# Emptying a group's accumulators before the next group's gate sums, and a new order of the last products

## The chip, the cores and the metric

The kernel runs on one core of a Trainium2 chip. The metric is device time in microseconds (us) from start to end of one execution. Of before, three runs are shown: median 794.53 us, from 793.96 to 796.04. Beside them stands one execution taken by the hardware profiler, which lasted 793.31 us; its trace spans 791.2 us from the first to the last instruction, and 2.1 us lie around it.

## What is computed

The reference runs three stages over 3072 tokens of 384 numbers: a recurrent attention, a mixture of eight experts with a skip score, and a dense feed-forward layer with a gate. Only the last is touched by the change:

```python
def _moe2_ref(x, w_in, w_out):          # x 3072x384, w_in 384x2048, w_out 2048x384
    h = x @ w_in
    g = h * (1.0 / (1.0 + np.exp(-h)))
    return (g @ w_out).astype(np.float32)
```

Sums are kept near float32 accuracy: each factor is split in a high and a low part (names ending in h and l), and a product is three matmuls, high by high, low by high and high by low (`product`, all at L934).

## The kernel before

The dense layer takes the tokens in six groups of 512. The 2048 inner columns are 16 blocks of 128. For each block f, `up` makes the sums of the gate (9 matmuls of 512 columns into a bank `ph`, two of which rotate), and `silu` makes the gate value g on ScalarE (L1201), its high part gh on ScalarE (L1202) and its low part gl on VectorE (L1203). I call that last step the gate subtraction.

Groups 0 and 1 then multiply plainly (`down`), into four banks y0 to y3, which `store` copies out at the end (L1371, two copies on VectorE and two on ScalarE), for an indirect store from GpSimd. These four banks are the ones that the next group needs.

Groups 2 to 5 (`seven`) save matmuls: blocks f = p and f = p + 8 form a pair, and of the product of a 2 by 2 arrangement (two blocks of the inner dimension, two halves of 256 tokens, two d tiles of the output) seven products are made in place of eight. For each pair, `pair` and `pair_split` make differences of gates and split them (VectorE L1215, L1224, L1226, ScalarE L1223; tiles tz and twd). TensorE then runs:

- `plain`: two products into the halves of bank y0 (3 matmuls of 256 columns each), `third` (the output's third d tile, which is multiplied plainly: 6 matmuls of 512 columns into bank `pd`) and a product of the gate's second half into y2[:, 1], with weights `sw`;
- `mixed`: four products, 12 matmuls of 256 columns, into both halves of y1, into y2[:, 0] and into y3[:, 0].

All eight pairs accumulate in the same banks. When the last pair is through, `out_plain` (ScalarE copy L1271, VectorE L1272), `out_third` (ScalarE L1276) and `out_mixed` (six VectorE additions, L1283 to L1288) combine the banks into the tile o, and `store` sends it off. Each pool tag y0 to y3 has one buffer, so the next group can't open a bank before the last reader of the same bank is through.

The order is written by times: `at(time, fn, ...)` puts a step in a list that is sorted by time, and each engine executes its own instructions in that order. Q is a group's start in these units, a pair takes PE_P = 7.44, and `lag` = Q + 8 PE_P is the start of the next group. The next group's block 0 is at `lag`, its block 8 at lag + PE_P/2 with its `silu` 2 later, `pair` at lag + PE_P/2 + 2.6 and `pair_split` at 3.2. In between stand the last pair's `plain` (lag + 1.9) and `mixed` (lag + PE_P/2 + 1.9), and `out_mixed` at lag + PE_P/2 + 3.3, that is, behind `pair_split` of the next group. In the last group (`end`), `third` of pairs 6 and 7 is taken out of `plain` and put behind the last `mixed`; its bank is copied out in two halves (L1278 on ScalarE, L1279 on VectorE), and two stores follow, both from SyncE's queue.

Of the kernel before, what the change touches and what calls it, by code (L numbers as in the profile page):

```python
# [949 lines left out]
def dense(tc, k, outer):  # L950
# [240 lines left out]
    def seven(g, Q, u, up):  # L1191
# [40 lines left out]
        def add(out, w, x, p, start, stop):  # L1232
            (wh, wl), (xh, xl) = w, x
            product(nc, out, [(wh, xh), (wl, xh), (wh, xl)], p == 0 and start, p == 7 and stop)
# [8 lines left out]
            u.y = [ps.tile([128, 2, 256], F32, name="py", tag="y%d" % n) for n in range(4)]  # L1243
            u.d = ps.tile([128, 512], F32, name="pd", tag="t", bufs=2)

        def plain(p):
            if p == 0:
                open_banks()
            add(u.y[0][:, 0], weights(p, 0), gate(p, 0), p, True, False)
            add(u.y[0][:, 1], weights(p + 8, 0), gate(p + 8, 0), p, False, True)  # L1250
            if not (end and p > 5):
                third(p)
            add(u.y[2][:, 1], sums(p, 3), gate(p + 8, 1), p, True, False)

        def third(p):
            for f in (p, p + 8):
                (wh, wl), xh, xl = weights(f, 2), u.gh[f], u.gl[f]
                product(nc, u.d, [(wh, xh), (wl, xh), (wh, xl)], f == 0, f == 15)

        def mixed(p):  # L1260
            add(u.y[1][:, 0], sums(p, 1), u.t[1], p, True, False)
            add(u.y[1][:, 1], sums(p, 2), u.t[2], p, False, True)
            add(u.y[2][:, 0], sums(p, 0), u.t[0], p, False, True)
            add(u.y[3][:, 0], weights(p + 8, 1), u.t[3], p, True, True)

        def half(j, n):
            return u.o[:, j, 256 * n:256 * n + 256]
# [4 lines left out]
            tt(half(0, 0), u.y[0][:, 1], half(1, 1), ALU.add)  # L1272

        def out_third():
            if not end:
                nc.scalar.copy(u.o[:, 2], u.d)  # L1276
                return
            nc.scalar.copy(half(2, 0), u.d[:, 0:256])  # L1278
            nc.vector.tensor_copy(half(2, 1), u.d[:, 256:512])  # L1279

        def out_mixed():
            p1 = half(1, 1)
            tt(half(0, 1), u.y[1][:, 0], p1, ALU.add)  # L1283
            tt(half(1, 0), u.y[1][:, 1], half(0, 1), ALU.add)
            tt(half(0, 1), u.y[2][:, 0], half(0, 1), ALU.add)
            tt(half(1, 1), u.y[2][:, 0], half(1, 0), ALU.add)
            tt(half(0, 1), u.y[2][:, 1], half(0, 1), ALU.add)
            tt(half(1, 0), half(1, 0), u.y[3][:, 0], ALU.subtract)  # L1288

        def store(a, b):  # L1290
            o = k.out[g * 512:g * 512 + 512, :].rearrange("n d -> (n d)").rearrange("(j p t) -> p j t", j=3, p=128)
            nc.sync.dma_start(o[:, a:b], u.o[:, a:b])

        u.g = [None, None]
        for p in range(8):
            t = Q + PE_P * p
            for i in range(2):
                at(t + PE_P * i / 2, up, p + 8 * i)
                at(t + PE_P * i / 2 + 2, silu, p + 8 * i)
            at(t + PE_P / 2 + 2.6, pair, p)  # L1300
            at(t + PE_P / 2 + 3.2, pair_split, p)
            at(t + PE_P + 1.9, plain, p)
            at(t + PE_P * 1.5 + 1.9, mixed, p)
        at(lag + 1.95, out_plain)
        at(lag + PE_P / 2 + 3.3, out_mixed)
        if not end:
            at(lag + 1.96, out_third)
            at(lag + PE_P, store, 0, 3)
            return
        at(lag + PE_P / 2 + 1.91, third, 6)  # L1310
        at(lag + PE_P / 2 + 1.92, third, 7)
        at(lag + PE_P, store, 0, 2)
        at(lag + PE_P + 0.1, out_third)
        at(lag + PE_P + 0.2, store, 2, 3)

    def group(g, Q):
        u = Ctx()
# [69 lines left out]
        for f in range(16):  # L1387
# [1 line left out]
            at(t, up, f)  # L1389
            at(t + 2, silu, f)  # L1390
            at(t + 2 * PE_F + 2, down, f)
        at(Q + 18 * PE_F, store)
    sw = {}
    order = k.const.tile([128, 8], U32, name="order")

# [364 lines left out]
```

## Time and profile before

| what | of before |
|---|---|
| median of three runs | 794.53 us (793.96 to 796.04) |
| profiled execution | 793.31 us, span of its trace 791.2 us |
| TensorE busy | 750.2 us, 95% of the span |
| VectorE, ScalarE, GpSimd busy | 536.6, 437.9 and 230.1 us |
| mean granted TensorE clock | 0.982 |
| the chain of work that ended last | TensorE 75%, VectorE 12%, DMA 6%, ScalarE 3% |

The busy time of TensorE counts matmuls from start to modelled end, and consecutive ones overlap; what to look for is where a stretch has idle time, and at which clock the matmuls behind it run. In the timeline rows below, the text in brackets gives how long the engine had been idle ahead of an instruction and whom it waited for. L numbers are lines of the kernel.

### The profile page before, as it was taken

The numbers are of one execution on the slowest core, as the hardware profiler recorded it, in microseconds if no ns is written. First come the engines' busy times: TensorE is split into PE (matmuls) and PEld (weight loads), VectorE is DVE, ScalarE is ACT, GpSimd is POOL, SyncE is SP. The second block draws the span as 40 slices with busy tenths as digits, with TensorE's granted clock in tenths as the row PEclk, the third lists the DMA queues.
The fourth block names the chain that finished last, engine by engine and source line by source line (L and its number), as shares of the span: only waits on it lengthen the run. The fifth ranks groups of instructions, "written<-read, shape, count | busy, mean of one in ns | idle before, by whom it ended". The sixth has DMA issues, their size and how long they took to land.

```text
span 791.2 us, 13883 instructions
## 1 busy us (share of the span) xinstructions
PE 750.2 (95%) x5471; PEld 686.1 (87%) x5471; DVE 536.6 (68%) x952; ACT 437.9 (55%) x718; POOL 230.1 (29%) x199
## 2 busy tenths in 40 slices
PE   2899999999989999999999999999999999999996
PEld 2799999998879999998899999978878887887884
DVE  7898899999556668679996345555555566465544
ACT  8899889954334554445774212345544454454543
POOL 5577657132536334452300148420000000000000
PEclk8699999999999999999999999999999999999998
DMA  8668685597659755566750010011010101101001
GB/s 341 182 184 272 223 294 177 176 255 219 210 186 327 274 192 180 199 235 205 239 161 1 20 61 1 1 41 41 1 41 1 41 1 40 41 1 41 1 1 44
DMA packets 31372, 101.88 MB, mean 129 GB/s; under 512 B 4929, under 2 KB 13249, under 8 KB 31297
## 3 DMA queue, kind: packets, MB, share of 16 engines
q1 hardware_dynamic: 26112, 88.31, 34.0%
q0 software_dynamic: 3072, 9.44, 3.3%
q10 hardware_dynamic: 2112, 3.15, 1.3%
q8 instruction: 45, 0.74, 0.4%
q14 instruction: 31, 0.25, 0.1%
HBM read 69.27 MB, written 12.58 MB: 103 GB/s over the span
## 4 chain that ended last, share of the span: by engine, by line
PE 75%; DVE 12%; DMA 6%; ACT 3%; issue 2%; SPq 2%; DVEq 0%; ACTq 0%
PE ph L934 29%; PE py L934 23%; PE pd L934 5%; PE sc L481 4%; DMA KQ<-o 4%; PE run L308 2%; PE pu L514 2%; PE py L499 2%; PE py L503 2%; SPq L445 1%; DMA raw<-in_w_dram 1%; PE tp L471 1%; PE ph L924 1%; DVE wl L1011 1%; DVE o L242 1%
## 5 line engine op out<-in xcount | busy, mean ns | idle before, releaser
L934 PE MATMUL ph<-cxh,wh 128*128 128x512 f32 x288 | 116.1, 403 | 0.0
L1203 DVE TENSOR_TENSOR gl<-g,gh 128x512 fp32r<-128x512 f32 x64 | 44.3, 692 | 103.4 <-ACT gh L1202 103.4
L934 PE MATMUL ph<-cxl,wh 128*128 128x512 f32 x288 | 114.3, 397 | 0.1
L934 PE MATMUL ph<-cxh,wl 128*128 128x512 f32 x288 | 114.2, 396 | 0.0
L1201 ACT ACTIVATE g<-ph 128x512 f32<-128x512 f32 x64 | 38.2, 597 | 68.8 <-PE ph L934 68.6
L934 PEld LDWEIGHTS ph<-cxl,wh 128*128 128x128 f32 x288 | 54.9, 191 | 13.2 <-DVE cxl L1344 0.5
L934 PEld LDWEIGHTS ph<-cxh,wl 128*128 128x128 f32 x288 | 55.2, 192 | 8.7
L934 PEld LDWEIGHTS ph<-cxh,wh 128*128 128x128 f32 x288 | 55.0, 191 | 8.4
L1223 ACT CAST tz<-twd 128x256 fp32r<-128x256 f32 x96 | 36.7, 407 | 36.8 <-DVE twd L1215 36.7
L481 PE MATMUL sc<-KQ 96*128 96x128 f32 x384 | 53.0, 286 | 1.0 <-DMA KQ<-o 0.8
L481 PEld LDWEIGHTS sc<-KQ 96*128 96x128 f32 x384 | 47.8, 198 | 3.3 <-issue 1.4
L1011 DVE TENSOR_TENSOR wl<-raw,wh 128x1536 fp32r<-128x1536 f32 x22 | 43.2, 1973 | 10.5 <-ACT wh L915 10.5
L915 ACT CAST wh<-raw 128x1536 fp32r<-128x1536 f32 x28 | 40.8, 1480 | 15.2 <-DMA raw<-in_w_dram 15.2
L934 PE MATMUL ph<-xh,wh 128*128 128x256 f32 x168 | 47.9, 285 | 0.0
L934 PE MATMUL ph<-xl,wh 128*128 128x256 f32 x168 | 47.6, 283 | 0.0
L934 PE MATMUL ph<-xh,wl 128*128 128x256 f32 x168 | 47.6, 283 | 0.0
L934 PE MATMUL py<-wh,gl 128*128 128x384 f32 x128 | 43.3, 338 | 0.0
L934 PE MATMUL py<-wh,gh 128*128 128x384 f32 x128 | 43.2, 338 | 0.0
L934 PE MATMUL py<-wl,gh 128*128 128x384 f32 x128 | 43.1, 336 | 0.0
L934 PE MATMUL py<-wh,hl 128*128 128x384 f32 x120 | 40.9, 341 | 2.2 <-DVE hl L929 2.1
L934 PE MATMUL py<-wh,hh 128*128 128x384 f32 x120 | 41.2, 344 | 0.2 <-ACT hh L1024 0.2
L1202 ACT CAST gh<-g 128x512 fp32r<-128x512 f32 x64 | 39.7, 621 | 2.0
(373 smaller groups left out, 2124.6 us busy)
## 6 DMA issues: line engine op xcount, KB each, us to landing
raw<-in_w_dram SPq DMA_DIRECT2D x30, 768.0 KB, 5.8
KQ<-o SPq DMA_DIRECT2D x40, 290.2 KB, 4.0
kq<-in_kq_dram SPq DMA_DIRECT2D x12, 768.0 KB, 5.5
a<-in_a_dram SPq DMA_DIRECT2D x10, 768.0 KB, 6.2
raw<-in_w_in_dram SPq DMA_DIRECT2D x8, 768.0 KB, 5.2
raw<-in_w_out_dram SPq DMA_DIRECT2D x8, 768.0 KB, 4.2
v<-in_v_dram SPq DMA_DIRECT2D x12, 384.0 KB, 6.1
xbuf<-xr SPq DMA_DIRECT2D x24, 192.0 KB, 3.3
```

The lines of the kernel that those rows point to most:

```text
L308: nc.tensor.matmul(p[:, i if bank is None else bank, g * CH:g * CH + CH], a[:, n * CH:n * CH + CH], tri, start=first and g == 0, stop=last ...
L481: nc.tensor.matmul(sc[:, j, :], key(4 * g + j), t.KQ[0:96, 4 * g + j, b, 1, 0:CH], start=True, stop=True)
L499: nc.tensor.matmul(py[64 * i:64 * i + 64, j, :], t.v[:, v0 + h * D:v0 + h * D + DP], u.P[:, h, :], start=True, stop=first)
L503: nc.tensor.matmul(py[64 * i:64 * i + 64, j, :], state[0:96, s0 + h * D:s0 + h * D + DP], t.KQ[0:96, h, b, 1, 0:CH], start=False, stop=True)
L514: nc.tensor.matmul(pu[:, h, 0:D], u.kn[:, h, :], t.v[:, v0 + h * D:v0 + h * D + D], start=not add or h == 0, stop=not add)
L915: nc.scalar.copy(hi, src)
L934: nc.tensor.matmul(out, a, x, start=first and n == 0, stop=last and n == len(pairs) - 1)
L1011: (nc.gpsimd if i == 3 and e > 1 else nc.vector).tensor_tensor(u.w[i][1], u.raw[i], u.w[i][0].bitcast(F32), ALU.subtract)
L1201: nc.scalar.activation(a, u.ph[f], AF.Silu)
L1202: nc.scalar.copy(u.gh[f], a)
L1203: tt(u.gl[f], a, u.gh[f].bitcast(F32), ALU.subtract)
L1223: nc.scalar.copy(h, u.x[:, n])
```

## The change

Four things are written differently. `plain` no longer holds the product into y2[:, 1]; it is now the last of `mixed`, and so y2 is opened by the product into its first half, with the flags for opening and closing exchanged. In groups 2 to 4, `out_mixed` moves from lag + PE_P/2 + 3.3 to lag + PE_P/2 + 1.91, right behind the last `mixed` and ahead of `silu` of the next group's block 8; its last two additions change places. In groups 0 and 1, `store` moves from Q + 18 PE_F to Q + 17 PE_F + 2.01 (PE_F = 3.84). In the last group, the third d tile of the last two pairs stands ahead of and between the parts of the last `plain`, ahead of the last `mixed`; its bank is copied out by one ScalarE instruction; and the output goes off in four stores, three on SyncE's queue and one on ScalarE's.

```diff
--- before.py
+++ after.py
@@ -1243,25 +1243,23 @@
             u.y = [ps.tile([128, 2, 256], F32, name="py", tag="y%d" % n) for n in range(4)]
             u.d = ps.tile([128, 512], F32, name="pd", tag="t", bufs=2)
 
-        def plain(p):
+        def plain(p, n=None):
             if p == 0:
                 open_banks()
-            add(u.y[0][:, 0], weights(p, 0), gate(p, 0), p, True, False)
-            add(u.y[0][:, 1], weights(p + 8, 0), gate(p + 8, 0), p, False, True)
-            if not (end and p > 5):
-                third(p)
-            add(u.y[2][:, 1], sums(p, 3), gate(p + 8, 1), p, True, False)
-
-        def third(p):
-            for f in (p, p + 8):
-                (wh, wl), xh, xl = weights(f, 2), u.gh[f], u.gl[f]
-                product(nc, u.d, [(wh, xh), (wl, xh), (wh, xl)], f == 0, f == 15)
+            for i in range(2) if n is None else [n]:
+                f = p + 8 * i
+                add(u.y[0][:, i], weights(f, 0), gate(f, 0), p, i == 0, i == 1)
+
+        def third(f):
+            (wh, wl), xh, xl = weights(f, 2), u.gh[f], u.gl[f]
+            product(nc, u.d, [(wh, xh), (wl, xh), (wh, xl)], f == 0, f == 15)
 
         def mixed(p):
             add(u.y[1][:, 0], sums(p, 1), u.t[1], p, True, False)
             add(u.y[1][:, 1], sums(p, 2), u.t[2], p, False, True)
-            add(u.y[2][:, 0], sums(p, 0), u.t[0], p, False, True)
+            add(u.y[2][:, 0], sums(p, 0), u.t[0], p, True, False)
             add(u.y[3][:, 0], weights(p + 8, 1), u.t[3], p, True, True)
+            add(u.y[2][:, 1], sums(p, 3), gate(p + 8, 1), p, False, True)
 
         def half(j, n):
             return u.o[:, j, 256 * n:256 * n + 256]
@@ -1272,11 +1270,7 @@
             tt(half(0, 0), u.y[0][:, 1], half(1, 1), ALU.add)
 
         def out_third():
-            if not end:
-                nc.scalar.copy(u.o[:, 2], u.d)
-                return
-            nc.scalar.copy(half(2, 0), u.d[:, 0:256])
-            nc.vector.tensor_copy(half(2, 1), u.d[:, 256:512])
+            nc.scalar.copy(u.o[:, 2], u.d)
 
         def out_mixed():
             p1 = half(1, 1)
@@ -1284,12 +1278,12 @@
             tt(half(1, 0), u.y[1][:, 1], half(0, 1), ALU.add)
             tt(half(0, 1), u.y[2][:, 0], half(0, 1), ALU.add)
             tt(half(1, 1), u.y[2][:, 0], half(1, 0), ALU.add)
+            tt(half(1, 0), half(1, 0), u.y[3][:, 0], ALU.subtract)
             tt(half(0, 1), u.y[2][:, 1], half(0, 1), ALU.add)
-            tt(half(1, 0), half(1, 0), u.y[3][:, 0], ALU.subtract)
-
-        def store(a, b):
+
+        def store(q, a, b, t=slice(0, 512)):
             o = k.out[g * 512:g * 512 + 512, :].rearrange("n d -> (n d)").rearrange("(j p t) -> p j t", j=3, p=128)
-            nc.sync.dma_start(o[:, a:b], u.o[:, a:b])
+            q.dma_start(o[:, a:b, t], u.o[:, a:b, t])
 
         u.g = [None, None]
         for p in range(8):
@@ -1299,19 +1293,24 @@
                 at(t + PE_P * i / 2 + 2, silu, p + 8 * i)
             at(t + PE_P / 2 + 2.6, pair, p)
             at(t + PE_P / 2 + 3.2, pair_split, p)
+            at(t + PE_P * 1.5 + 1.9, mixed, p)
+            if end and p > 5:
+                continue
             at(t + PE_P + 1.9, plain, p)
-            at(t + PE_P * 1.5 + 1.9, mixed, p)
-        at(lag + 1.95, out_plain)
-        at(lag + PE_P / 2 + 3.3, out_mixed)
+            for i in range(2):
+                at(t + PE_P + 1.91, third, p + 8 * i)
         if not end:
+            at(lag + 1.95, out_plain)
             at(lag + 1.96, out_third)
-            at(lag + PE_P, store, 0, 3)
+            at(lag + PE_P / 2 + 1.91, out_mixed)
+            at(lag + PE_P, store, nc.sync, 0, 3)
             return
-        at(lag + PE_P / 2 + 1.91, third, 6)
-        at(lag + PE_P / 2 + 1.92, third, 7)
-        at(lag + PE_P, store, 0, 2)
-        at(lag + PE_P + 0.1, out_third)
-        at(lag + PE_P + 0.2, store, 2, 3)
+        at(lag - PE_P + 1.9, plain, 6)
+        for d, fn, a in ((0, third, (6,)), (0, third, (14,)), (1, plain, (7, 0)), (1, third, (7,)), (2, plain, (7, 1)),
+                         (2.1, out_plain, ()), (2.2, store, (nc.sync, 0, 1, slice(0, 256))), (2.3, third, (15,)),
+                         (2.4, out_third, ()), (2.5, store, (nc.sync, 2, 3)), (6, out_mixed, ()),
+                         (6.1, store, (nc.scalar, 1, 2)), (6.2, store, (nc.sync, 0, 1, slice(256, 512)))):
+            at(lag + d, fn, *a)
 
     def group(g, Q):
         u = Ctx()
@@ -1389,7 +1388,7 @@
             at(t, up, f)
             at(t + 2, silu, f)
             at(t + 2 * PE_F + 2, down, f)
-        at(Q + 18 * PE_F, store)
+        at(Q + 17 * PE_F + 2.01, store)
     sw = {}
     order = k.const.tile([128, 8], U32, name="order")
 
```

VectorE at the border from group 2 to group 3, before (with what each row waits for; o<-py are the additions of `out_mixed`, gl the gate subtractions, twd and tz the differences and splits of the next group's first pair):

```order
L1224 TENSOR_TENSOR tz<-twd,tz 128x256 [waits PE_49,Activation_49]
L1224 TENSOR_TENSOR tz<-twd,tz 128x256 [waits Activation_49] x2
L1226 TENSOR_TENSOR twd<-twd,g 128x256 [waits DVE_49]
L1224 TENSOR_TENSOR twd<-twd 128x256 [waits Activation_49]
L1283 TENSOR_TENSOR o<-py,o 128x256
L1284 TENSOR_TENSOR o<-py,o 128x256 [waits DVE_49]
L1285 TENSOR_TENSOR o<-py,o 128x256 [waits DVE_49]
L1286 TENSOR_TENSOR o<-py,o 128x256
L1287 TENSOR_TENSOR o<-py,o 128x256 [waits DVE_49]
L1288 TENSOR_TENSOR o<-o,py 128x256 [waits DVE_49]
L1203 TENSOR_TENSOR gl<-g,gh 128x512 [waits Activation_49] x2
```

The first row is the next group's first split; both gate subtractions of that pair stand ahead of it, and the additions follow the whole splitting.

The same place after the change:

```order
L1203 TENSOR_TENSOR gl<-g,gh 128x512 [waits Activation_49]
L1277 TENSOR_TENSOR o<-py,o 128x256 [waits PE_49]
L1278 TENSOR_TENSOR o<-py,o 128x256 [waits DVE_49]
L1279 TENSOR_TENSOR o<-py,o 128x256 [waits DVE_49,PE_49]
L1280 TENSOR_TENSOR o<-py,o 128x256
L1281 TENSOR_TENSOR o<-o,py 128x256 [waits DVE_49]
L1282 TENSOR_TENSOR o<-py,o 128x256
L1203 TENSOR_TENSOR gl<-g,gh 128x512 [waits Activation_49]
L1215 TENSOR_TENSOR twd<-g 128x256
L1215 TENSOR_TENSOR twd<-g,twd 128x256 [waits DVE_49]
L1215 TENSOR_TENSOR twd<-g 128x256
L1224 TENSOR_TENSOR tz<-twd,tz 128x256 [waits Activation_49] x3
```

The six additions have moved from behind the splitting to between the two gate subtractions, and the third of them, the first to read y2, now waits for TensorE.

TensorE at the very end, before (py are the banks y0 to y3, pd the third d tile; rows with sw and gh are the product into y2[:, 1], rows with tz and twd the other mixed products):

```order
L934 MATMUL py<-gh,sw 128x256 x2
L934 MATMUL py<-gl,sw 128x256
L934 MATMUL py<-tz,sw 128x256 x3
L934 MATMUL py<-tz,wh 128x256
L934 MATMUL py<-tz,wl 128x256
L934 MATMUL py<-tz,wh 128x256
L934 MATMUL py<-tz,sw 128x256 x3
L934 MATMUL py<-twd,wh 128x256
L934 MATMUL py<-twd,wl 128x256
L934 MATMUL py<-twd,wh 128x256
L934 MATMUL pd<-gh,wh 128x512
L934 MATMUL pd<-gh,wl 128x512
```

After the change, from the last `plain`'s first part on:

```order
L934 MATMUL py<-gh,wh 128x256
L934 MATMUL py<-gh,wl 128x256
L934 MATMUL py<-gl,wh 128x256
L934 MATMUL pd<-gh,wh 128x512
L934 MATMUL pd<-gh,wl 128x512
L934 MATMUL pd<-gl,wh 128x512
L934 MATMUL py<-gh,wh 128x256
L934 MATMUL py<-gh,wl 128x256
L934 MATMUL py<-gl,wh 128x256
L934 MATMUL pd<-gh,wh 128x512
L934 MATMUL pd<-gh,wl 128x512
L934 MATMUL pd<-gl,wh 128x512
```

Products of the third d tile that stood behind the last mixed products now stand ahead of them, between the parts of the last `plain`.

## Rows read from the trace of the kernel before

**Rows 1.** Waits of TensorE from 500 us on: engine, line, releaser; total, times, longest.

```profile
PE py L934 <- DVE o L1287: 5.4, 3, 1.8
PE py L934 <- DVE o L1371: 1.8, 1, 1.8
```

**Rows 2.** Windows of TensorE inside group 3: length, busy (instructions), clock, DMA share, GB/s.

```profile
592.12:649.54 57.42, 57.42 (x328) 1.00 0.05 14
```

**Rows 3.** Timeline of TensorE, groups 2 to 3: start, length, engine, line, instruction [idle].

```profile
580.45 0.52 PE L934 MATMUL py<-tz,sw 128*128 128x256 f32 x3
...
588.01 0.50 PE L934 MATMUL py<-gh,sw 128*128 128x256 f32 x2 [1.81 <-DVE o L1287]
...
592.12 0.52 PE L934 MATMUL py<-tz,sw 128*128 128x256 f32 x3
...
600.13 0.52 PE L934 MATMUL py<-tz,sw 128*128 128x256 f32 x3
```

**Rows 4.** Timeline of VectorE at the border from group 2 to 3.

```profile
581.93 0.69 DVE L1203 TENSOR_TENSOR gl<-g,gh 128x512 fp32r<-128x512 f32 x1 [1.24 <-ACT gh L1202]
...
585.97 0.41 DVE L1283 TENSOR_TENSOR o<-py,o 128x256 f32<-128x256 f32 x1
...
587.55 0.41 DVE L1287 TENSOR_TENSOR o<-py,o 128x256 f32<-128x256 f32 x1
...
588.21 0.68 DVE L1203 TENSOR_TENSOR gl<-g,gh 128x512 fp32r<-128x512 f32 x1
```

**Rows 5.** Timeline of TensorE, first mixed products around the border from group 3 to 4.

```profile
649.54 0.52 PE L934 MATMUL py<-tz,sw 128*128 128x256 f32 x3
...
659.65 0.52 PE L934 MATMUL py<-tz,sw 128*128 128x256 f32 x3
```

**Rows 6.** The same around the border from group 4 to 5.

```profile
717.08 0.52 PE L934 MATMUL py<-tz,sw 128*128 128x256 f32 x3
...
728.75 0.52 PE L934 MATMUL py<-tz,sw 128*128 128x256 f32 x3
```

**Rows 7.** Windows of TensorE over the sums behind the three waits (columns as rows 2).

```profile
588.40:591.90 3.50, 3.50 (x12) 0.51 0.58 225
...
657.50:659.60 2.10, 2.10 (x11) 1.00 0.61 239
...
725.20:728.40 3.20, 3.20 (x9) 0.50 0.64 244
```

**Rows 8.** Timeline of TensorE and VectorE at the border from group 1 to 2.

```profile
513.78 0.69 DVE L1203 TENSOR_TENSOR gl<-g,gh 128x512 fp32r<-128x512 f32 x1 [3.44 <-ACT gh L1202]
...
517.75 1.01 DVE L1371 COPY o<-py 128x384 f32<-128x384 f32 x2
...
516.25 0.40 PE L934 MATMUL ph<-cxl,wh 128*128 128x512 f32 x1
518.45 0.35 PE L934 MATMUL py<-gh,wh 128*128 128x256 f32 x1 [1.80 <-DVE o L1371]
```

**Rows 9.** Timeline of all engines at the end of the kernel.

```profile
775.43 0.52 PE L934 MATMUL py<-tz,sw 128*128 128x256 f32 x3
...
778.89 0.95 PE L934 MATMUL py<-tz,sw 128*128 128x256 f32 x3 [0.49 <-ACT tz L1223]
...
780.61 0.43 DVE L1224 TENSOR_TENSOR twd<-twd 128x256 fp32r<-128x256 f32 x1 [0.53 <-ACT twd L1223]
...
783.70 1.75 SPq L1292 DMA_DIRECT2D out_dram<-o  x2
783.82 0.39 PE L934 MATMUL pd<-gl,wh 128*128 128x512 f32 x1
...
784.65 0.42 DVE L1279 COPY o<-pd 128x256 f32<-128x256 f32 x1 [0.98 <-ACT o L1278]
```

**Rows 10.** DMA issues, last two stores: queue, count, KB, us from issue to landing.

```profile
out_dram<-o SPq DMA_DIRECT2D x1, 512.0 KB, 2.7
out_dram<-o SPq DMA_DIRECT2D x1, 256.0 KB, 4.1
```

## The prediction, made before the changed kernel was run

> **What bounds the kernel now.** I read the waits of TensorE first, then its timeline around the places they name, then what stood on VectorE there. Within a group TensorE has no idle time: from the first mixed products of group 3 to its last ones, 57.42 us of 57.42 us are busy at full clock [rows 2]. So in the second half TensorE sets the time, and whatever is to be gained there lies between groups and at the very end. At the three borders between two seven-product groups TensorE waits 1.8 us each for an addition on VectorE (L1287), and once as long, at the border from group 1 to group 2, for a copy (L1371) [rows 1]. A reader should look at what VectorE did meanwhile: it was not late because it is slow, but because of its order. At the border from group 2 to group 3 the operands of `out_mixed` were complete when the mixed products ended (start 580.45 and twelve narrow products, 1.4 us [rows 3]); VectorE began it only at 585.97 [rows 4], after the gate subtraction of the next group's block 8 (581.93) and all of that pair's splitting.
>
> **Unit costs.** A full pair takes 600.13 - 592.12 = 8.01 us [rows 3] and holds 24 matmuls of 512 columns and 21 of 256, so 8.01 / 34.5 = 0.232 us for a wide one and 0.116 us for a narrow one.
>
> **The change part by part.** No matmul is added or removed; the last `out_third` becomes one ScalarE copy in place of two, and the last stores are cut differently.
>
> *Borders 2 to 3, 3 to 4, 4 to 5.* The distance from one set of mixed products to the next is 592.12 - 580.45 = 11.67 us [rows 3], 659.65 - 649.54 = 10.11 us [rows 5] and 728.75 - 717.08 = 11.67 us [rows 6], against 8.01 within a group: losses of 3.66, 2.10 and 3.66 us. The waits are alike. What differs is the clock behind them: it was granted at 0.51 and 0.50 (1.2 GHz) over the next sums at two borders and at 1.00 (2.4 GHz) at the third [rows 7]. In each case TensorE had been idle just before. Without the wait I expect no fall, since no stretch without an idle time shows one [rows 2].
>
> Does the wait go, or what comes late next? Two edits act. The fifth mixed product, which opens bank y2, goes behind the other mixed products, so the next group first asks for y2 nine wide and six narrow products, 2.8 us, later. And `out_mixed` goes ahead of the next group's block-8 subtraction on VectorE. The price is that this subtraction, the pair's differences and its splits now queue behind six additions, and ScalarE's casts and next activation behind those. Worked out at the first border: three narrow products that stood before the mixed ones now stand behind them, so these start at 580.45 - 0.35 = 580.10 and the last of fifteen starts at 581.72 and is done at about 582.0. The row order gives the third addition a wait on TensorE and the last one none, so I take it that both halves of y2 have to be finished before the third addition begins, at 582.05. Four additions at 0.33 us (587.55 to 588.21 is two [rows 4]) put the block-8 subtraction at 583.4 and its end, 0.69 us later, at 584.07; before it started at 581.93, so everything behind it is 1.45 us later. TensorE reaches the product that needs it after nine wide sums from 581.84 (583.93) and five narrow products: 584.51. Margin 0.44 us. The pair's splits, finished at 585.97 before, finish at 587.4; their first user starts at 580.10 + 8.01 = 588.11. So both are in time, the first narrowly, and the three borders give back 3.66 + 2.10 + 3.66 = 9.42 us. Ends: if the clock falls anyway, 9.42 - 2 x 1.56 = 6.3 us; if a residual idle of up to 0.7 us returns at each border, 2.1 us less again.
>
> By the Trainium skill, page "PSUM — Partial Sum Buffer", section "PSUM bank collisions raise a hardware error", two engines may not be in one bank at the same time, even at disjoint columns, so waits must go by bank. That speaks against placing the fifth product last in a bank that is read next: with waits by half bank the subtraction would come about 0.2 us earlier and the margin would be 0.6 us. No row of before shows a read of one half during a write of the other. The sum is 9.42 us by either; by the page the late subtraction, rival (a), is the likelier, and without it I would give that rival half its chance.
>
> *Border 1 to 2.* TensorE's last sum starts at 516.25, lasts to 516.48, and the next product starts at 518.45 [rows 8]: 1.97 us lost, no slow clock. The copies that it waits for come at 517.75 on VectorE, behind the pair's splitting. They move up behind the block-8 subtraction, which ends at 513.78 + 0.69 = 514.47; two copies take 1.01 us [rows 8], so VectorE is through at 515.5, ScalarE with its two before that. The bank is asked for at 516.48: a margin of 1 us, and 1.97 us gained. The pair's splitting comes 1 us later, and its user comes 4.2 us after 516.48 (six wide, six narrow, nine wide), at 520.65. That delay costs nothing. The indirect stores on GpSimd start earlier, and nothing waits for them. Bounds: 0 to 1.97.
>
> *The end.* TensorE waits 0.5 us for a split before the last mixed products and a little more within them [rows 9], then runs twelve wide products until 783.82 + 0.39. Now all twelve stand ahead of the last mixed products, around the two parts of the last plain product, and cover the splits. From 775.43 - 0.35 = 775.08: fifteen narrow (1.74) to 776.82, twelve wide and six narrow (3.48) to 780.30, fifteen narrow to 782.04, done at 782.2. The last split, 780.61 + 0.43 - 0.35 = 780.7, is needed at 780.30 + 1.04 = 781.34: hidden. TensorE ends 2.0 us earlier, but the chain behind it is longer: four additions after the last matmul (782.25 to 783.7) in place of one copy. Before, the last copy ended at 784.65 + 0.42 = 785.07 and its store followed. So the last store moves from 785.1 to 783.7: 1.4 us, if its landing takes as long. Before, it took 4.1 us behind the other store and that one 2.7 us [rows 10]; now the last is half as large and shares the time with one store from ScalarE's queue. I keep the same landing, as the nearest row, with bounds of 1.4 us either side: 0 to 2.8 us gained.
>
> *The new order within pairs.* The block-(p+8) gate parts are now read by the mixed products too, and VectorE's subtraction got a wait on TensorE for the buffer. At the first border the buffer's last reader is the set of mixed products that ends some 8 us before those of 580.45, at about 574.4 with the moved three; the subtraction stands at 581.93 or later [rows 4]. That margin of 7 us makes it free.
>
> **The sum.** 9.42 + 1.97 + 1.4 = 12.8 us from the profiled execution's 793.31 us (span 791.2): 780.5 us. The median of the runs is 1.22 us above that execution, which would give 781.7; but the extra time of other runs may be further slow-clock stretches behind the gaps, which would go as well. I forecast 781.0 us.
>
> **The rivals.** (a) *The subtraction is late.* If a wait on TensorE costs VectorE 0.15 us more at each step, the 0.44 us margin is gone; TensorE then idles up to 0.7 us at three borders, and if the clock falls as before at two, 2.1 + 3.1 = 5.2 us of the gain is lost: 786 us. For it: the margin is the smallest of all; against: it would need all additions slower than the rows show. (b) *The slow stretches don't hang on the gaps*: at two of four equal gaps none followed [rows 7, 8]. Then 3.1 us stay: 784 us. Against: none lies elsewhere. (c) *The wait is only renamed*: TensorE waits for another bank opened at the same point, since the group takes all four banks at once. Then only the end gains: 792 us. Against: before, the product that waited was the one into y2, behind those into y0 [rows 3], so banks are waited for one by one. (d) *Slower:* the new wait on gate buffers binds in every pair, so that the block-8 subtraction follows the mixed products and holds up the next sums. At 32 pairs the 12.8 us are used up at 0.40 us a pair; at 0.6 us the kernel would take 800 us. Against: the 7 us margin above.
>
> **How the numbers follow.** Forecast 0.77, (a) 0.10, (b) 0.07, (c) 0.04, (d) 0.02. From 0.3%, 2.4 us, a difference can be told from none here. Forecast, (a) and (b) are all faster by more: 0.94; (c) is the same: 0.04; (d) slower: 0.02. The range goes from 778.3 (780.5, less 1.4 for the end at its best bound, less 0.8 for the spread of runs) to 785.2, which takes in (b), half of (a) and the end at no gain.
>
> **What would show it.** TensorE's waits should no longer name additions of `out_mixed` or the copies of the plain groups; mixed products at borders should follow each other at 8.0 us; the granted clock should be 1.00 from 523 us to the last matmul; the last matmuls should be narrow ones, ending some 2 us earlier relative to the last group's start, and the last store should be issued about 1.4 us earlier. It is wrong if a wait for a gate subtraction (L1203) appears on TensorE just behind each border, if half-clock stretches remain, or if the last landings take longer than 4 us.

## The result, and the profile after

The changed kernel takes 783.41 us (median of four runs, 782.21 to 785.54) beside 795.28 us for the kernel before (four runs, 793.96 to 797.16): a ratio of 0.9852, with an interval of 0.9819 to 0.9885. The profiled execution took 784.44 us. It is faster by well over 0.3%, as forecast, and the time lies in the range; it is 2.4 us above the forecast of 781.0 us.

First the page of the changed kernel: its span, TensorE's busy line, and the granted clock in 40 slices.

```profile
span 782.3 us, 13899 instructions
...
PE 743.9 (95%) x5471; PEld 683.3 (87%) x5471; DVE 537.4 (69%) x951; ACT 438.3 (56%) x718; POOL 230.1 (29%) x199
...
PEclk9899999999999999999999999999999999999998
```

TensorE's busy time fell from 750.2 to 743.9 us although no matmul was removed. About half of these 6.3 us, 2 x 1.56, are the same matmuls run at half clock behind two of the waits [rows 7]; the rest is spread over borders, pairs and the end. The view of TensorE's waits from 500 us on, which named L1287 and L1371 before [rows 1], has no row left. The windows over the groups (columns as in rows 2) are busy throughout at full clock:

```profile
520.00:600.00 80.00, 80.00 (x459) 1.00 0.08 31
600.00:660.00 60.00, 60.00 (x344) 1.00 0.08 27
660.00:770.00 110.00, 110.00 (x627) 1.00 0.04 15
```

The timeline of TensorE at the border from group 2 to group 3 answers to rows 3 (start, length, engine, line, instruction):

```profile
582.13 0.52 PE L934 MATMUL py<-tz,sw 128*128 128x256 f32 x3
...
583.79 0.29 PE L934 MATMUL py<-gl,sw 128*128 128x256 f32 x1
...
586.55 0.28 PE L934 MATMUL py<-gl,wh 128*128 128x256 f32 x1
...
590.09 0.52 PE L934 MATMUL py<-tz,sw 128*128 128x256 f32 x3
```

Mixed products now follow each other at 590.09 - 582.13 = 7.96 us across the border, where it was 11.67. The fifth product ends the set (583.79). VectorE at the same place answers to rows 4:

```profile
583.03 0.42 DVE L1277 TENSOR_TENSOR o<-py,o 128x256 f32<-128x256 f32 x1 [0.28 <-PE py L934]
...
584.11 0.42 DVE L1279 TENSOR_TENSOR o<-py,o 128x256 f32<-128x256 f32 x1 [0.20 <-PE py L934]
584.45 0.42 DVE L1280 TENSOR_TENSOR o<-py,o 128x256 f32<-128x256 f32 x1
584.90 0.42 DVE L1281 TENSOR_TENSOR o<-o,py 128x256 f32<-128x256 f32 x1
...
585.58 0.68 DVE L1203 TENSOR_TENSOR gl<-g,gh 128x512 fp32r<-128x512 f32 x1
```

VectorE now waits for TensorE there (0.28 and 0.20 us), not the other way round. The block-8 gate subtraction ends at 585.58 + 0.68 = 586.26; TensorE reads it at 586.55, so 0.29 us are left. The third addition (584.11) reads the first half of y2, and yet it began only when the fifth product, which writes the second half, had ended (583.79 + 0.29 = 584.08). By the Trainium skill, page "PSUM — Partial Sum Buffer", section "PSUM bank collisions raise a hardware error", two engines may not be in one bank at the same time, even at disjoint columns. The trace agrees: the read began 0.03 us behind the end of the write.

The border from group 1 to group 2 on VectorE and TensorE answers to rows 8:

```profile
518.70 1.01 DVE L1370 COPY o<-py 128x384 f32<-128x384 f32 x2
...
520.56 0.39 PE L934 MATMUL ph<-cxl,wh 128*128 128x512 f32 x1
520.79 0.28 PE L934 MATMUL py<-gh,wh 128*128 128x256 f32 x1
```

The copies are through at 519.71, 1.08 us before TensorE asks for the bank, and the narrow product starts 0.23 us behind the last gate sum, in place of 2.20.

And the end, on SyncE's queue, TensorE, VectorE and ScalarE's queue, which answers to rows 9:

```profile
766.91 0.52 PE L934 MATMUL py<-tz,sw 128*128 128x256 f32 x3
...
772.88 3.17 SPq L1286 DMA_DIRECT2D out_dram<-o  x3
...
773.82 0.29 PE L934 MATMUL py<-gl,sw 128*128 128x256 f32 x1
...
774.14 0.42 DVE L1279 TENSOR_TENSOR o<-py,o 128x256 f32<-128x256 f32 x1 [0.19 <-PE py L934]
...
775.27 0.42 DVE L1282 TENSOR_TENSOR o<-py,o 128x256 f32<-128x256 f32 x1
775.38 0.37 ACTq L1286 DMA_DIRECT2D out_dram<-o  x1
```

**Where the time went.** The spans differ by 791.2 - 782.3 = 8.9 us only. To see the change alone, I cut each span at the start of the last gate sum ahead of group 2's first narrow product (516.25 before [rows 8], 520.56 after). What lies behind the cut, the *stage*, holds all that the change touches but the copies of group 0. The *end* begins with pair 6's mixed products in the last group (775.43 [rows 9] and 766.91):

| us | before | after | gain |
|---|---|---|---|
| ahead of the cut | 516.25 | 520.56 | -4.31 |
| cut to group 2's first mixed products | 6.78 | 4.37 | 2.41 |
| three borders | 11.67 + 10.11 + 11.67 | 7.96 + 7.97 + 7.97 | 9.55 |
| the 27 steps from pair to pair inside groups | 218.95 | 218.08 | 0.87 |
| end | 15.77 | 15.39 | 0.38 |
| stage | 274.95 | 261.74 | 13.21 |

The fifth product (0.35 us) stood ahead of the mixed products before and ends them now, so 0.35 us have passed from the second row to the last: the border from group 1 to 2 gave 2.06 us in truth and the end 0.73. The stage gave 13.2 us, and a longer first part hid 4.3 of it. That difference is not the change's: it is there in full at the first gate sum of the dense layer (373.22 us before, 377.54 after), ahead of everything that the diff touches.

### The profile page after: what moved, and what is told of

Same layout as the page of the kernel before. It is cut to its first block, busy times and chain, and to the rows that moved or that the text cites. A ratio compares the mean times of both kernels' runs of the same rounds, so it can differ in the third digit from the quotient of the medians.

```text
span 782.3 us, 13899 instructions
## 1 busy us (share of the span) xinstructions
PE 743.9 (95%) x5471; PEld 683.3 (87%) x5471; DVE 537.4 (69%) x951; ACT 438.3 (56%) x718; POOL 230.1 (29%) x199
## 4 chain that ended last, share of the span: by engine, by line
PE 74%; DVE 9%; DMA 8%; SPq 3%; ACT 3%; issue 2%; POOL 0%; DVEq 0%; ACTq 0%
PE ph L934 30%; PE py L934 25%; PE pd L934 6%; SPq L445 3%; PE sc L481 3%; DMA KQ<-o 3%; DMA kq<-in_kq_dram 3%; DMA raw<-in_w_dram 2%; PE run L308 2%; PE py L499 1%; PE pu L514 1%; PE py L503 1%; DVE wl L1011 1%; PE tp L471 1%; DVE o L242 1%
## 5 line engine op out<-in xcount | busy, mean ns | idle before, releaser
L934 PE MATMUL ph<-cxh,wh 128*128 128x512 f32 x288 | 113.6, 395 | 0.0
L934 PE MATMUL ph<-cxh,wl 128*128 128x512 f32 x288 | 112.6, 391 | 0.0
```

The lines of the kernel that those rows point to most:

```text
L934: nc.tensor.matmul(out, a, x, start=first and n == 0, stop=last and n == len(pairs) - 1)
```

## The experiments

**The two kernels again.** No edit; both run once more.

> The kernel before, unchanged, a second time. The profiles of before and of the changed kernel differ by 4.3 us ahead of the dense layer's first seven-product group, in a part that neither edit touches (the last sum ahead of the first narrow product starts at 516.25 us before and at 520.56 us after). Theory: that is variation from execution to execution; then this point falls anywhere within some 4 us of 516 to 520 us here too, the ratio to the kernel before is 1.000 within 0.3%, and from that point to the end of the span it is 274.9 us again, within 1.6 us for one slow stretch of the clock more or less. Rival: the changed kernel is slower ahead of its changes; then this point is at 516 us again, within 1 us, and that of the changed kernel stays near 520.

> The changed kernel a second time. Theory (the gain is borders, copies, end, and all else is variation): from the last sum ahead of the first narrow product to the end of the span 261.7 us again, within 0.5 us, granted clock 1.00 there; ratio to the kernel before 0.983 to 0.986. Rival (4 us are lost ahead of the changes): the same stretch is 261.7 us, but the point ahead of it is at 520 us or later again.

Measured: before again 796.36 us (twelve runs; ratio 1.0003, 0.9980 to 1.0026), after again 782.47 us (six runs; ratio 0.9836, 0.9806 to 0.9866). The spans of the profiles are 796.2 and 780.0 us. The timeline of TensorE at the cut, of before again and then of after again:

```profile
521.41 0.40 PE L934 MATMUL ph<-cxl,wh 128*128 128x512 f32 x1
```

```profile
518.77 0.39 PE L934 MATMUL ph<-cxl,wh 128*128 128x512 f32 x1
```

Stages: 796.2 - 521.41 = 274.8 us and 780.0 - 518.77 = 261.2 us, within 0.5 us of the first pair of profiles, while the first part of the same code came out 5.2 us longer for before and 1.8 us shorter for after. The first part varies from one execution to the next; the stage repeats within 0.5 us.

**The additions ahead, alone.** The kernel before with one line changed:

```diff
-        at(lag + PE_P / 2 + 3.3, out_mixed)
+        at(lag + PE_P / 2 + (3.3 if end else 1.91), out_mixed)
```

> The kernel before, with only the six additions of out_mixed moved ahead of the next group's block-8 gate subtraction at the three borders between seven-product groups; the fifth product stays in plain, the copies of the plain groups and the end are as before. Theory of a redundant pair (either edit alone frees y2 in time): the bank is free at about 583.4 in the clock of the kernel before and asked for at 586.0; no wait at the three borders, border distances 8.0 us, 9.4 us less than before: ratio 0.988. Rival (both edits are needed): TensorE still waits about 1 us or more at each border and the gain is under 5 us, ratio 0.994 or more.

Measured: 788.14 us (ratio 0.9895, 0.9861 to 0.9930). Waits of TensorE from 500 us on, and the window behind the one long wait:

```profile
PE py L934 <- DVE o L1371: 1.8, 1, 1.8
...
```

```profile
521.30:525.30 4.00, 4.00 (x16) 0.57 0.12 49
```

All three borders came to 8.01 us: this edit alone takes their waits away. The gap at group 1 to 2, untouched, was followed by the half clock this time (0.57 in the mean of 4 us, and 1.6 us lost), which it was not in before. The stage is 267.1 us, 7.8 us less than before; without the slow stretch 9.4.

**The fifth product last, alone.** In the kernel before, with the flags for opening and closing y2 and the last two additions exchanged, too (`...` stands for lines left out here and below):

```diff
 def plain(p):
...
-            add(u.y[2][:, 1], sums(p, 3), gate(p + 8, 1), p, True, False)
...
 def mixed(p):
...
+            add(u.y[2][:, 1], sums(p, 3), gate(p + 8, 1), p, False, True)
```

> The kernel before, with only the product into y2[:, 1] moved behind the other mixed products (and the last two additions exchanged); the additions stay behind the next group's splitting. Theory of a redundant pair: y2 is freed at about 588.3 in the clock of the kernel before and asked for at 588.8, y1 is freed at 586.9 and asked for at 588.1; no wait at the three borders: 9.4 us less, and a pair shorter by some 0.04 us as in the changed kernel, 1.2 us over all: ratio 0.987. Rival (both are needed): a wait of 0.5 us or more at each border with half-clock stretches behind some, ratio 0.992 or more.

Measured: 786.11 us (ratio 0.9891, 0.9857 to 0.9926). Waits of TensorE from 500 us on, and the window behind the first of them:

```profile
PE py L934 <- DVE o L1371: 1.8, 1, 1.8
...
```

```profile
518.70:522.70 4.00, 4.00 (x21) 1.00 0.12 49
```

The three borders are 7.97 us each, so this edit alone suffices too. In this kernel the additions still stand behind the splitting, but y2 is asked for later. VectorE's last addition, the last to read y2, and TensorE's next product into y2, the third of the next mixed ones:

```profile
587.59 0.42 DVE L1288 TENSOR_TENSOR o<-py,o 128x256 f32<-128x256 f32 x1
...
588.64 0.51 PE L934 MATMUL py<-tz,sw 128*128 128x256 f32 x3
```

The bank is free 588.64 - 588.01 = 0.63 us before it is written. Each pair takes 7.97 us in place of 8.01 (but for two steps in each group, 8.45 and 8.9 us in every kernel here), which the additions alone did not bring. The gap at group 1 to 2 is as long as in the run above, and no slow stretch follows. Stage 265.2 us.

**The end, alone.** The changed kernel with the borders as before: fifth product first outside the last group, additions at 3.3, copies of groups 0 and 1 late.

```diff
+            if not end:
+                at(t + PE_P + 1.92, fifth, p)
...
-            at(lag + PE_P / 2 + 1.91, out_mixed)
+            at(lag + PE_P / 2 + 3.3, out_mixed)
...
-        at(Q + 17 * PE_F + 2.01, store)
+        at(Q + 18 * PE_F, store)
```

> The kernel before with only the new end: in the last group the fifth product is last in mixed, the third d tile of the last two pairs stands ahead of and between the last plain product, one ScalarE copy, four stores on two queues. Borders and copies as before. The term of the prediction is 1.4 us. The traces of the changed kernel give 0.7 and 1.2 us for it: from the start of the mixed products of the last pair but one to the end of the span 15.4 and 14.9 us, where the kernel before takes 15.7 us and starts these products 0.35 us later in its pair. Theory (the term is smaller since the landing behind the last issue became longer): 14.9 to 15.4 us here, the last store issued some 1.4 us earlier against the last sums than before, and landing 0.3 to 0.6 us later after its issue. Rival (the term is right, the rest was variation): 14.6 us or less.

Measured: 795.55 us in one run, beside 795.43 for before. Waits of TensorE, and the windows behind them:

```profile
PE py L934 <- DVE o L1286: 4.5, 2, 2.3
PE py L934 <- DVE o L1376: 1.8, 1, 1.8
```

```profile
522.00:526.00 4.00, 4.00 (x16) 0.61 0.12 49
594.00:597.00 3.00, 3.00 (x11) 0.59 0.67 262
663.50:666.50 3.00, 3.00 (x10) 0.54 0.67 262
```

The end took 14.94 us, as the theory said; in before it was 15.77, which makes 16.12 with the moved product. But the theory's reason doesn't show in this trace: SyncE's last issue ended 9.14 us behind pair 6's mixed products, 1.23 us earlier than the 10.37 of before with the moved product, and the span went on for 5.8 us behind it, as long as in before. The whole is nonetheless as slow as before, and for reasons outside the end: the two old borders wait 2.3 us, because the last two additions stay exchanged and the one that frees y2 is now the sixth, and all three gaps were followed by a slow stretch. Only the border from group 4 to 5, where the new order applies, has no gap. In this one trace, pairs before it take 8.01 us and pairs behind it 7.97: the 0.04 us go with the place of the fifth product, not with the execution.

**Delays of 0.9 and 2.3 us on VectorE.** The changed kernel with idle additions between the six additions and the subtraction; a delay of the first kind and one of the second:

```diff
+        def hold_up():
+            for _ in range(2):              # second kernel: range(5)
+                tt(k.fill, k.fill, k.fill, ALU.add)
...
+            at(lag + PE_P / 2 + 1.92, hold_up)
```

> The changed kernel with two added VectorE additions of 256 columns on a spare tile, each on the result of the one before (0.45 us each by the spacing of dependent additions), between out_mixed and the next group's block-8 gate subtraction at the three borders between seven-product groups: 0.9 us. In the changed kernel the subtraction ends at 586.26 us and its product starts at 586.55: a margin of 0.29 us. Theory (that margin is what is left, as rival a of the prediction has it): TensorE waits for a gate subtraction (L1203) about 0.6 us at each of the three borders, 1.8 us in all, more where a slow stretch of the clock follows. Rival (there is more cover than that): no wait, the same 261.5 us from the last sum ahead of the first narrow product to the end.

> The same with five added additions: 2.25 us. Theory: a wait of about 1.95 us at each border, 5.9 us in all. If the slow stretches of the clock are a consequence of such a gap, whatever makes the gap, one or two of the three borders are followed by half clock over the next products, 1.5 us each: border distances of 9.9 us where none follows and some 11.5 us where one does, and 261.5 + 5.9 + 1.5 to 3 = 269 to 270.5 us to the end. If they belonged to the old order or to something else, all three distances are 9.9 us at full clock, and 267.4 us.

Measured: 781.88 and 788.94 us, one run each. Waits of TensorE of the first, then of the second, and then windows that begin right behind the second's three waits:

```profile
PE py L936 <- DVE gl L1205: 1.2, 3, 0.4
```

```profile
PE py L936 <- DVE gl L1205: 5.3, 3, 1.8
```

```profile
586.10:589.50 3.40, 3.40 (x16) 1.00 0.01 4
653.30:656.70 3.40, 3.40 (x16) 1.00 0.02 7
720.60:724.00 3.40, 3.40 (x9) 0.52 0.02 5
```

With 0.9 us each border takes 8.62 us, 0.65 more than 7.97, so the margin was about 0.25 us, close to the 0.29 of the trace. With 2.3 us two borders take 10.02 and 10.01 us and the third, with a slow stretch behind it (0.52 in the mean of 3.4 us), 11.60; the stage is 269.2 us, as forecast for one slow stretch. This puts the gap back by another road, with another waiting product and another releaser, and the slow stretch comes back with it, at one border of three. A reading hint: the waits listed are 0.40 and 1.78 us where the borders lost 0.65 and 2.05. The view counts from the modelled end of the matmul ahead, and consecutive matmuls overlap by some 0.25 us; the distance between two like instructions is the safer number.

**Narrow products together.** To see where the 0.04 us a pair come from: the kernel with the additions ahead, and the fifth product directly behind the plain ones, ahead of `third`. It has as few changes from narrow to wide as the changed kernel. (The line that moves the additions, shown above, is left out.)

```diff
             add(u.y[0][:, 1], weights(p + 8, 0), gate(p + 8, 0), p, False, True)
+            add(u.y[2][:, 1], sums(p, 3), gate(p + 8, 1), p, True, False)
             if not (end and p > 5):
                 third(p)
-            add(u.y[2][:, 1], sums(p, 3), gate(p + 8, 1), p, True, False)
```

> The kernel before with the additions moved early at the borders (as the run that moved them alone), and with the product into y2[:, 1] ahead of the third d tile instead of behind it, so that a pair's narrow products of plain stand together: a pair then changes between matmuls of 256 and 512 columns four times, as in the changed kernel, and not six times as before. A pair takes 7.97 us in the changed kernel and 8.01 us before, which the prediction did not have. Theory (each narrow product between wide ones costs some 0.04 us): 7.97 us a pair. Rival (it comes from the place behind the mixed products): 8.01 us. At the borders y2 is asked for 1.4 us earlier than with the additions alone, at about 584.6 in the clock of before, where it is free at about 583.4: no wait there by either.

Measured: 786.89 us in one run. TensorE's timeline, one pair in group 3:

```profile
591.85 0.52 PE L934 MATMUL py<-tz,sw 128*128 128x256 f32 x3
...
599.84 0.40 PE L934 MATMUL py<-tz,sw 128*128 128x256 f32 x2
```

7.99 us, and 7.98 to 8.00 in the other pairs outside the longer steps; the three borders take 7.99 us too, with no wait. My theory fell: this order gives 0.02 us, not 0.04. The rest goes with the fifth product's place behind the mixed ones. What the trace adds is where the time lies. Counted between the starts of their neighbours, the nine gate sums of a block take in the median 2.07 us (behind the fifth product) or 2.08 (behind the mixed products) in before, and 2.04 in both places after. In this run they take 2.04 us behind the third d tile and still 2.08 directly behind the mixed products, so half of the gain is there. Of the 2 x 0.03 to 0.04 us, the changed kernel gives back 0.02, since its fifth product takes 0.37 us in place of 0.35. Why the sums take more or less stays open.

**The copies of groups 0 and 1, alone.** The kernel before with one line changed:

```diff
-        at(Q + 18 * PE_F, store)
+        at(Q + 17 * PE_F + 2.01, store)
```

> The kernel before with one edit: the copies of groups 0 and 1 (and their store) stand at Q + 17 PE_F + 2.01. Theory: the four copies of group 1 come 2 us earlier, and TensorE starts group 2's narrow products 0.23 us after the last wide sum has started, as in the changed kernel, where before it took 2.20; from that sum to group 2's first mixed product 4.8 us in place of 6.78, the other three borders stay at 10.1 to 11.7 us, so the stretch from that sum to the end is about 2.0 us shorter than the 274.8 to 274.95 of the kernel before. Rival: the four copies are late with a neighbour that the other edits had cleared away (the additions or the fifth product); then the wait at L1371 is only smaller than 1.8 us, and the stretch is shorter by under 1 us.

Measured: 790.84 us in one run, beside 796.16 for before. TensorE at the cut, its waits, and the windows behind the three of them:

```profile
517.77 0.39 PE L934 MATMUL ph<-cxl,wh 128*128 128x512 f32 x1
518.01 0.28 PE L934 MATMUL py<-gh,wh 128*128 128x256 f32 x1
```

```profile
PE py L934 <- DVE o L1287: 5.4, 3, 1.8
```

```profile
588.00:592.00 4.00, 4.00 (x26) 1.00 0.51 197
655.30:658.50 3.20, 3.20 (x10) 0.50 0.63 246
724.50:728.00 3.50, 3.50 (x23) 1.00 0.59 224
```

The first gap is gone (0.24 us) and 2.02 us with it (6.78 to 4.76 from the cut to the mixed products). The stage is 270.9 us, 4.0 less than before. Two of these are the edit, and 1.6 come from the slow stretches behind the old waits: one here (borders 10.09, 11.66, 10.08), two in before. The remaining 0.3 us lie at the end.

**A version meant to beat both.** The changed kernel with another order in the last pair: one product of the third d tile behind the mixed ones, so that the additions run beside it. Left out of the diff: in the last pair the product into y3 and its subtraction come last.

```diff
...
-(2.2, store, (nc.sync, 0, 1, slice(0, 256))), (2.3, third, (15,)),
-(2.4, out_third, ()), (2.5, store, (nc.sync, 2, 3)), (6, out_mixed, ()),
-(6.1, store, (nc.scalar, 1, 2)), (6.2, store, (nc.sync, 0, 1, slice(256, 512)))
+(2.2, store, (nc.sync, 0, 1, slice(0, 256))), (5.7, third, (15,)),
+(6, out_mixed, ()), (6.1, store, (nc.sync, 0, 1, slice(256, 512))), (6.15, out_third, ()),
+(6.2, store, (nc.sync, 1, 2)), (6.3, store, (nc.scalar, 2, 3))
```

> The changed kernel with a new order in the last pair alone: the second block's product of the third d tile (3 wide matmuls, 0.7 us) stands behind the last mixed products, the product into y3 is the last of the mixed ones and its subtraction the last addition; the stores are half of tile 0, then its other half and tile 1 on SyncE's queue, and tile 2 on ScalarE's. Theory: the additions that read y2 run beside the last products, and behind TensorE's end only one ScalarE copy and a store stand in the chain; from the first mixed product of the last pair but one to the span's end 14.2 to 14.7 us against 14.9 to 15.4 of the changed kernel, the rest unchanged, so 0.5 to 0.9 us less. Rival: the time from the last store's issue to the span's end, 6.1 to 6.6 us so far, goes with the number and size of the stores that end together, and takes the gain back: 14.9 to 15.4 us again.

> The changed kernel once more, beside the run ahead of it. Theory: the stretch from the last wide sum ahead of group 2's narrow products to the end 261.2 to 261.8 us, with 14.9 to 15.4 us of it behind the first mixed product of the last pair but one; the part ahead of that sum anywhere from 516 to 521 us, so that the whole time moves by up to 5 us with no change in the code. Rival: the part ahead goes with the code (its addresses or its length), and is again 518.8 to 520.6 us, the two values seen with this kernel so far.

Measured: 782.62 us (0.984, 0.980 to 0.988) and, for the changed kernel beside it, 782.42 (0.9838, 0.9797 to 0.9879). The end of the new version, VectorE, SyncE's queue and ScalarE's, and then, of the changed kernel beside it, TensorE at the cut and SyncE's queue:

```profile
770.81 2.90 SPq L1290 DMA_DIRECT2D out_dram<-o  x3
...
772.68 0.41 DVE L1284 TENSOR_TENSOR o<-o,py 128x256 f32<-128x256 f32 x1
...
772.70 0.38 ACTq L1290 DMA_DIRECT2D out_dram<-o  x1
```

```profile
518.54 0.39 PE L934 MATMUL ph<-cxl,wh 128*128 128x512 f32 x1
...
770.85 3.18 SPq L1286 DMA_DIRECT2D out_dram<-o  x3
```

The last store was issued at 770.81 + 2.90 = 773.7, 0.3 us earlier than in the changed kernel (774.0), but both spans end at 780.0, and the end takes 15.15 and 15.11 us. My theory (14.2 to 14.7 us) fell, and the time is what the rival said: the time behind the last issue, 6.3 us here and 6.0 there, took the gain back. Whether the stores caused that is not shown, since the same time is 5.8 to 6.2 us over six traces with one and the same end. No version beat the changed kernel. Its stage was 261.5 us, within 0.3 of the two before, and the cut came at 518.54, just outside the two values seen with this code. In the trace of the short delay, nearly the same code, it came at 516.47: code alone does not set it.

## Why the prediction held, point by point

**The borders** were forecast at 9.42 us and gave 9.55. Rival (c), the wait only renamed, is out: no wait is left. Two edits act on them, and the prediction took them together; the runs showed that either alone removes all three waits. With the fifth product last alone there was no wait, and with the additions ahead alone there was none either. The pair of them adds no time at the borders, and no margin over the fifth product alone, which left 0.63 us: the subtraction had 0.29 us with both edits, at each border, and 0.17 us with the additions alone (its end at 587.95 + 0.69 = 588.64, its product at 588.81).

**The slow clock** was taken to hang on the gaps. In the changed kernel no gap is left and every window behind the borders is at 1.00; with the gap put back by a delay, a slow stretch was there again. Over all thirteen profiles ten slow stretches lie between the cut and TensorE's last matmul, each at one of the gaps of 1.8 or 2.3 us. Rival (b) is out. But the prediction could not say when a gap is followed by half clock, and I still can't: of 18 gaps of 1.8 us in eight profiles, 8 were followed by a slow stretch and 10 were not, at the same place in one run and not in another. Of before, this is the window behind the gap at group 1 to 2, where rows 8 show no clock; the same gap was followed by 0.57 with the additions alone:

```profile
518.70:522.70 4.00, 4.00 (x23) 1.00 0.13 51
```

**The margin** of rival (a) was 0.29 us, not 0.44, and it sufficed: the rival is out. The mis-sized term is the four additions at 0.33 us: L1281 starts 0.45 us behind L1280, so four take 585.58 - 584.11 = 1.47 us, not 1.35, and the third addition came 0.03 us later. The two additions that the 0.33 was read from [rows 4] don't wait for the one just before them; L1281 does, since it overwrites what L1280 reads, and that comes from the exchange of the last two. The delay of 0.9 us put its price on record: with the margin used up, each border pays what is beyond it.

**The border from group 1 to 2** was forecast at 1.97 us and gave 2.06, and 2.02 alone.

**The end** was forecast at 1.4 us and gave 0.73. Up to the issue of the last store the chain went nearly as worked out. From pair 6's mixed products to the end of SyncE's last issue it was 783.70 + 1.75 - 775.43 = 10.02 us in before [rows 9], 10.37 with the moved product, and is 772.88 + 3.17 - 766.91 = 9.14 now: 1.23 us earlier, not 1.4. What failed is the step from there to the end, "I keep the same landing", and not because the landing took longer. These are the last store's issue and landing (us from issue to landing at the end) in the changed kernel, and the landing with the fifth product last alone, which has the old stores:

```profile
775.71 0.33 SPq L1286 DMA_DIRECT2D out_dram<-o  x1
...
out_dram<-o SPq DMA_DIRECT2D x1, 128.0 KB, 3.4
```

```profile
out_dram<-o SPq DMA_DIRECT2D x1, 256.0 KB, 4.0
```

The smaller last store landed 3.4 us behind its issue, at 779.1, where it was 4.1 in before, at 785.1 + 4.1 = 789.2 [rows 10]. But the span ended 3.1 us behind that landing, and 2.0 us behind it in before; with the fifth product last alone (issue at 774.75) it was 2.8. So the end of the span doesn't follow the last landing by a fixed time, as the sum took it to without saying so. Counted from SyncE's last issue, the span went on for 5.75 us in before and 6.25 after; over the five profiles with the old end and the old order of products it is 5.4 to 5.75 us, over the six with the new end 5.8 to 6.25. With the means, 5.6 and 6.0, the end is worth 0.9 us. That the new stores make it longer is not shown: the longest of all, 6.4 us, is the kernel with the fifth product last alone, with the old two stores. What sets it stays open.

**Not in the sum** were the pairs: 0.87 us over 27 steps, 0.04 us in most. I had priced the moved product at nothing, since no matmul is removed; the trace of before does not show that the sums would take 2.04 us in place of 2.07 and 2.08 with other products ahead of them.

**Rival (d)** is out: no new wait inside pairs.

**The total.** The stage gave 13.2 us where the sum had 12.8: the misses of -0.7 at the end and +0.9 inside pairs nearly cancel, and that is luck. Between medians of runs the gain was 11.9, 14.7 and 13.7 us, each time with the first part's variation in it. That the time was 2.4 us above the forecast has another cause, which the sum can't hold: the level it was taken from. In the thirteen profiles the cut lies anywhere from 516.25 to 521.41 us, and the profiled execution of before, with 516.25, was at the lowest end. Its first part of 516.25 us and a stage after of 261.5, with 2.1 around, would make 779.9; with the changed kernel's own cuts, 518.54 to 520.56, they make 782.1 to 784.2, and the three medians measured, 782.42 to 783.41, lie there. What in the first part makes it longer or shorter is not settled here: no run changed anything there.

## What to carry to other kernels

Where two bank users meet at a border, look at the order on the engine that empties them before asking for a faster engine: here moving six additions ahead of a later split, or asking for the bank 2.8 us later, was each enough, and the second alone left more to spare (0.63 us) than both together (0.29). Price a gap of TensorE at its length (here 1.8 us) and, as a chance, at nearly as much again for the clock that may follow it (1.6 us, in 8 of 18 cases). When a change sits late in a kernel, cut the span at a point ahead of it and compare what lies behind: the first part of this one varies by 5 us, more than a third of the gain.

## What the runs showed of the hardware

- A gap of 1.8 us on TensorE, of one length and at like places, was followed by half clock (0.50 to 0.61 over the next 3 to 4 us) in 8 of 18 cases, with about 1.6 us lost in each; both gaps of 2.3 us were, and none of the three of 0.4 us.
- A block of nine wide sums took 2.07 to 2.08 us or 2.04 us by the order of the products ahead: 2.08 directly behind the mixed products (before, and narrow products together), 2.04 where the fifth product stood between (after).
- Between the end of SyncE's last issue and the end of the span lay 5.4 to 6.4 us in the thirteen profiles, and it didn't go with the landing of the last store: this took 4.1 us in before and 3.4 in the changed kernel, and the span ended 2.0 and 3.1 us behind it. In one pair of traces, issuing the last store 0.3 us earlier moved the end by nothing.
